# A first-stage subtraction moved behind memsets, a reordered first gate, the first job's splits moved to its second half, and a new order list

## The chip, the cores and the metric

The kernel runs on one core of a Trainium2 chip. The metric is the time of one execution on the device, in microseconds (us); of several runs the median counts. Engines are named as in the profile: PE is TensorE's matmuls (PEld its weight loads), DVE is VectorE, ACT is ScalarE, POOL is GpSimd, SP issues most DMAs.

## What is computed

One block of 2048 tokens with 512 features goes through attention with 32 heads of 16 columns that share one key and one value head, and through a gated feed-forward layer (FFN) with 1376 hidden columns. A gate per token mixes the two.

```python
g = sigmoid((x * gate_w).sum(-1, keepdims=True))
q = (x @ wq).reshape(B, S, 32, 16)           # 32 heads
k, v = x @ wk, x @ wv                        # one head
p = softmax(einsum("bhqd,bkd->bhqk", q, k) * 16 ** -0.5)
a = einsum("bhqk,bkd->bhqd", p, v).reshape(B, S, 512) @ wo
b = (gelu(x @ w_gate) * (x @ w_up)) @ w_down
out = g * a + (1 - g) * b
```

## The kernel before

Everything that needs fp32 accuracy is done as a product of a high and a low half: a tile `t` becomes `hi` (a rounding cast) and `lo = t - hi` (a subtraction), and a product is three matmul passes, high by high, low by high, high by low. Making the two halves is called a split. In the steady part DVE does the cast and POOL the subtraction (`split`, L179 to L184, called by `split_part`, L349).

**First stage (prologue, L159 to L480).** The four groups of 512 tokens are worked one after the other. For each, `first_passes` (L383) runs one 12-matmul pass for the first gate tile `gf` (which also holds the key columns) and one for the first up tile `uf` (value columns), and then 48 matmuls give the queries (`pq`). For the first group, `xh`/`xl` are the halves of its x (four chunks of 128 features), `gh0`/`gl0` those of the weights; `gl0[:, 1]`, the low half for `uf`, is made by POOL at L230, between the memsets of small constants. POOL then clears `hot` (L231 to L233), the tile `zz` (a view of 32 rows of `woh`, L235, L236), and sends `zz` out by four DMAs.

**Steady part (L866 on).** The order of the work on PE is written out by hand, in the list `PLAN`: one line for each FFN or output job, which `play` (L837) reads word by word. `S0`, `S1`, `S2` issue two score matmuls into one of three two-bank PSUM tiles `pair0` to `pair2` and one exponential of both on ACT (L751); `S` issues one score matmul into `single`. The scores of neighbouring heads use the two halves of PE's rows and run side by side. `V`n multiplies n steps of 128 keys by the values (L819; a step is eight PE instructions, on four column groups at once). `H`n opens the line's job in tile `pair`n, `F`n runs n of its steps, each two matmuls on the two halves of PE's rows, and `R` closes it. `T` advances the activation of the last gate job.

A job (`pair_mm`, L507) has two halves, since the two row halves exchange their banks in between: the first matmul of the second half waits for a no-op on POOL (L523), called the relay here, which waits for the last matmuls of the first half. POOL's instructions run in the order of the program, so the relay also stands behind what was queued on POOL ahead of it. After every third step of a job one waiting piece of side work is taken (`slot`, L488): splits for the next job, from the list `todo`, at the third and sixth step of the first half and the third, sixth and ninth of the second; pieces of the softmax's division (`bg`) also at the other places.

A gate job ends in `gelu` (L537): DVE copies `g` from the job's PSUM tile into `gs` (L541), reads `u` from it (L542), does two more operations (L546, L547), ACT a tanh (L550), DVE an operation (L553) and the split of the result (L557, L558). The tile is free for scores again after L542. At the first `V` of all, everything that is left of the activation is flushed, so that ACT's tanh stands ahead of the exponentials that follow. `gates` (L861: one tanh on ACT, then two small DVE operations at L863 and L864) comes once, with the sixth word `S` of the list.

Of the kernel before, what the change touches and what calls it, by code (L numbers as in the profile page):

```python
# [9 lines left out]
F32 = mybir.dt.float32  # L10
# [21 lines left out]
KR = 48  # L32
QK = 51
# [74 lines left out]
]  # L108


@with_exitstack
def mix_kernel(ctx, tc, xT, wq, wo, wf, out):
    nc = tc.nc
    cp = ctx.enter_context(tc.tile_pool(name="cp", bufs=1))
    dr = ctx.enter_context(tc.tile_pool(name="dr", bufs=1, space=DRAM))
    ps_a = ctx.enter_context(tc.tile_pool(name="ps_a", bufs=1, space=PSUM))
    ps_f = ctx.enter_context(tc.tile_pool(name="ps_f", bufs=1, space=PSUM))
    ctx.enter_context(tc.manual_schedule())
# [457 lines left out]
    def gate_job(n):  # L576
        tg, r = chunks[n]

        def begin():
            flush(todo)  # L580
            queue_parts(parts(n))
            return weights_terms(n, 0), weights_terms(n, 1)
# [346 lines left out]
```

## Time and profile before

| | us |
|---|---|
| median of 3 runs | 1224.77 (1224.66 to 1225.57) |
| profiled execution | 1225.59 |
| its span, first to last instruction | 1223.8 |
| PE busy | 1215.6 |
| ACT busy | 1030.4 |
| DVE busy | 528.5 |
| POOL busy | 214.8 |

Times in the trace count from the start of the span. The profile's view of 40 slices shows the granted clock at 9 (90% or more) in all of them. The matmul ends are modelled and overlap: what a matmul costs is the distance from its start to the next one's start, not its own duration.

### The profile page before, as it was taken

How to read it: one execution, taken by the hardware profiler on the slowest of the kernel's cores; microseconds unless marked ns; L12 is line 12 of the kernel's file. 1: busy time of each engine (PE TensorE's matmuls, PEld its weight loads, DVE VectorE, ACT ScalarE, POOL GpSimd, SP SyncE). 2: the span in 40 equal slices, each digit the busy share in tenths (PEclk: the TensorE clock that was granted, in tenths of full speed). 3: DMA queues.
4: the chain of work that ended last, by engine and by line, in shares of the span. 5: the costliest groups of instructions: out<-in, count | busy, mean ns of one | idle time of the engine just before them, and what ended most of it. 6: DMA issues, size and time to landing. Idle time of an engine off the chain costs nothing.

```text
span 1223.8 us, 23880 instructions
## 1 busy us (share of the span) xinstructions
PE 1215.6 (99%) x9742; PEld 684.2 (56%) x9742; DVE 528.5 (43%) x812; ACT 1030.4 (84%) x1301; POOL 214.8 (18%) x188
## 2 busy tenths in 40 slices
PE   9999999999999999999999999999999999999998
PEld 6874555555554565455555555555554555555555
DVE  7773532555245331445426333263616234144524
ACT  5549988888889888989888987889889989799983
POOL 5412201222121100212112110121312011012100
PEclk9999999999999999999999999999999999999999
DMA  8632101212012100112212120112312111011000
GB/s 335 208 131 73 53 8 49 66 53 88 23 53 67 49 32 23 47 52 69 73 36 66 32 75 23 32 38 64 84 43 72 32 58 41 23 40 45 24 1 35
DMA packets 39841, 73.93 MB, mean 60 GB/s; under 512 B 5488, under 2 KB 5744, under 8 KB 39728
## 3 DMA queue, kind: packets, MB, share of 16 engines
q1 hardware_dynamic: 39184, 71.32, 19.1%
q8 instruction: 77, 1.26, 0.4%
q0 software_dynamic: 256, 0.79, 0.2%
q14 instruction: 36, 0.29, 0.1%
q10 hardware_dynamic: 288, 0.26, 0.1%
HBM read 57.41 MB, written 14.94 MB: 59 GB/s over the span
## 4 chain that ended last, share of the span: by engine, by line
PE 92%; ACT 0%; DVE 0%; issue 0%; DVEq 0%; POOL 0%; ACTq 0%; POOLq 0%
PE acc L819 38%; PE pair L515 30%; PE pair L746 20%; PE single L746 3%; PE pair L499 1%; ACT ring L751 0%; PE u L499 0%; DVE acc L628 0%; PE single L499 0%; ACT gs L550 0%; DVE t L553 0%; DVE gs L547 0%; DVE gs L541 0%; DVE t L542 0%; DVEq L925 0%
## 5 line engine op out<-in xcount | busy, mean ns | idle before, releaser
L751 ACT ACTIVATE ring<-pair 128x1024 f32<-128x1024 f32 (+1 forms) x944 | 879.6, 992 | 125.4 <-PE pair L746 123.1
L819 PE MATMUL acc<-ring,v 128*32 128x512 f32 x4096 | 480.9, 597 | 0.0
L746 PE MATMUL pair<-Q,kp 51*128 51x512 f32 x1794 | 389.6, 421 | 0.5 <-ACT ring L751 0.4
L746 PEld LDWEIGHTS pair<-Q,kp 51*128 51x128 f32 x1794 | 201.6, 185 | 203.0 <-ACT ring L751 140.0
L819 PEld LDWEIGHTS acc<-ring,v 128*32 128x32 f32 x4096 | 115.1, 109 | 245.7 <-issue 238.3
L184 POOL TENSOR_TENSOR gl<-st,gh 128x512 fp32r<-128x512 f32 x80 | 112.8, 1430 | 752.2 <-DVE gh L183 433.5
L515 PE MATMUL pair<-xh,gh 64*128 64x512 f32 x624 | 167.5, 393 | 1.1 <-POOLq L523 1.1
L515 PE MATMUL pair<-xh,gl 64*128 64x512 f32 x624 | 167.9, 391 | 0.0
L515 PE MATMUL pair<-xl,gh 64*128 64x512 f32 x624 | 167.1, 391 | 0.0
L751 ACT ACTIVATE ring<-single 128x512 f32<-128x512 f32 x254 | 155.2, 611 | 7.3 <-PE single L746 6.8
L541 DVE COPY gs<-pair 128x512 f32<-128x512 f32 x39 | 27.0, 692 | 207.4 <-PE pair L515 180.9
L515 PEld LDWEIGHTS pair<-xl,gh 64*128 64x128 f32 x624 | 94.5, 186 | 11.0
L746 PE MATMUL single<-Q,kp 51*128 51x512 f32 x254 | 100.4, 395 | 0.0
L515 PEld LDWEIGHTS pair<-xh,gl 64*128 64x128 f32 x624 | 94.8, 186 | 9.5
L515 PEld LDWEIGHTS pair<-xh,gh 64*128 64x128 f32 x624 | 93.9, 186 | 10.3 <-POOLq L523 1.5
L515 PE MATMUL pair<-dl,hh 64*128 64x512 f32 x352 | 91.7, 392 | 0.0
L515 PE MATMUL pair<-dh,hh 64*128 64x512 f32 x352 | 91.2, 393 | 0.0
L515 PE MATMUL pair<-dh,hl 64*128 64x512 f32 x352 | 91.0, 392 | 0.0
L184 POOL TENSOR_TENSOR dl<-st,dh 128x512 fp32r<-128x512 f32 x44 | 57.2, 1302 | 129.7 <-PE pair L746 84.4
L784 DVE RECIPROCAL nz<-n 128x128 f32<-128x128 f32 (+1 forms) x62 | 57.1, 952 | 0.5
L761 DVE COPY n<-acc 128x512 f32<-128x512 f32 x16 | 11.1, 692 | 103.4 <-PE acc L819 103.4
L515 PEld LDWEIGHTS pair<-dl,hh 64*128 64x128 f32 x352 | 51.7, 186 | 6.6 <-issue 0.8
(154 smaller groups left out, 1052.1 us busy)
## 6 DMA issues: line engine op xcount, KB each, us to landing
st<-wf SPq DMA_DIRECT2D x125, 256.0 KB
scr<-q SPq DMA_DIRECT2D x16, 512.0 KB
Q<-scr SPq DMA_DIRECT2D x64, 128.0 KB
Q<-scr SPq DMA_DIRECT2D x64, 64.0 KB
out<-acc SPq DMA_DIRECT2D x16, 256.0 KB
xr<-xT SPq DMA_DIRECT2D x6, 512.0 KB
st<-xT SPq DMA_DIRECT2D x12, 256.0 KB
xr<-xT SPq DMA_DIRECT2D x4, 256.0 KB
```

Source lines behind the costliest of these rows:

```text
L184: eng_l.tensor_sub(lo, src, hi)
L499: nc.tensor.matmul(ps, a, b, start=(first and q == 0), stop=(last and q == len(terms) - 1), skip_group_check=True)
L515: mm = nc.tensor.matmul(ps, a[rs], b[rs], start=(half == 0 and q == 0), stop=(half == 1 and q == len(X) - 1), skip_group_check=True)
L541: nc.vector.tensor_copy(gs, g)
L746: nc.tensor.matmul(ps[:, i * TG : (i + 1) * TG], kp[rs, kc * P : (kc + 1) * P], Q[u][rs, h // 2], start=True, stop=True)
L751: nc.scalar.activation(ring[:, to * TG : (to + b - a) * TG], ps[:, a * TG : b * TG], AF.Exp, bias=0.0, scale=SCALE)
L761: nc.vector.tensor_copy(c0, ac)
L784: nc.vector.reciprocal(z[:, cs], r[:, cs])
L819: nc.tensor.matmul(accp[u][32 * j : 32 * j + 32], vt[:, kc], ring[:, k * TG : (k + 1) * TG], start=(kc == 0), stop=(kc == NKC - 1), skip_g ...
```

## The change

It has five parts.

- POOL's subtraction for `gl0[:, 1]` moves from ahead of `hot` to behind the clearing of `zz`, and that is cut from one memset of four quarters to two of one quarter each (the third quarter is set to 1 as before, the fourth is not sent out and no longer cleared).
- The first gate pass takes its twelve matmuls in the order of a table, `FIRST` of (chunk, kind), where kind 0 is high by high, 1 low weights, 2 low x: the low halves of chunks 1 and 2 come later. All four groups use it.
- The split of `d2` (the down weights of hidden tile 2) is no longer done ahead of the list, but queued with the first gate job (n = 2).
- Two empty pieces are put ahead of it in `todo`, so that this job's three splits (`d2`, and the two of `g3`, the next gate weights) fall to its second half.
- All lines of `PLAN` are other ones; the kinds of jobs and their number (55 `f`, 6 `w`) stay. Lines 1 and 2 are shown.

```diff
+FIRST = [(0, 0), (0, 1), (0, 2), (1, 0), (1, 1), (2, 0), (2, 1), (1, 2), (3, 0), (3, 1), (2, 2), (3, 2)]
 PLAN = [
-    "t: S0 S1 T S",
-    "f: H2 F12 S0 S1 F5 S0 F S F2 S1 F4 R S0 S V S1 S0 T S2 V3 S1 S0 S2 V2 S1",
+    "t: S0 S1",
+    "f: H2 F9 S0 F3 S S1 F2 S0 F S F6 S1 F3 R S0 S V S1 S0 T S2 V3 S1 S0 S2 V2 S1",
...
     make_identity(nc, ident)
-    nc.gpsimd.tensor_sub(gl0[:, 1], g0[1], gh0[:, 1])
     nc.gpsimd.memset(hot, 0.0)
     for r in (QK - 1, 64 + QK - 1):
         nc.gpsimd.memset(hot[:, r : r + 1], 1.0)
     zz = woh[0:H]
-    nc.gpsimd.memset(zz.bitcast(F32), 0.0)
+    nc.gpsimd.memset(zz[:, 0].bitcast(F32), 0.0)
+    nc.gpsimd.memset(zz[:, 1].bitcast(F32), 0.0)
+    nc.gpsimd.tensor_sub(gl0[:, 1], g0[1], gh0[:, 1])
     nc.gpsimd.memset(zz[:, 2].bitcast(F32), 1.0)
...
         if t == 0:
-            seq = [(a, b, c) for c in range(NC) for a, b in kinds]
+            seq = [(*kinds[k], c) for c, k in FIRST]
...
         def begin():
             flush(todo)
+            if n == 2:
+                todo.extend([lambda: None] * 2)
+                queue_parts([("d", 2, 0)])
             queue_parts(parts(n))
...
     chain.pop(0)()
-    split_part(("d", 2, 0))
     defer(5, gates)
```

What stands in a row on POOL in the first stage, after the setting up of `ident` (`gl0` and `gh0` are the weights' halves, `st0` their source, `woh` is where `zz` lies). Before:

```order
masks.py:199 AFFINE_SELECT ident_120<-ident_120 128x128
L230 TENSOR_TENSOR gl0_119<-st0_103,gh0_118 128x512
L231 MEMSET hot_84 1x128
L233 MEMSET hot_84 1x1 x2
L235 MEMSET woh_88 32x2048
L236 MEMSET woh_88 32x512
L238 DMA shs_69<-woh_88 96x1x512 x4
```

and after the change:

```order
masks.py:199 AFFINE_SELECT ident_120<-ident_120 128x128
L231 MEMSET hot_84 1x128
L233 MEMSET hot_84 1x1 x2
L235 MEMSET woh_88 32x512
L236 MEMSET woh_88 32x512
L237 TENSOR_TENSOR gl0_119<-st0_103,gh0_118 128x512
L238 MEMSET woh_88 32x512
L240 DMA shs_69<-woh_88 96x1x512 x4
```

The subtraction has moved behind four memsets, and the large memset has become a quarter, twice.

What stands in a row on DVE around the first gate job of the list (`dh2` and `gh3` are the casts of the splits, `gc` and `gt` the gates, `hh1` and `hl1` the split of hidden tile 1, `gs2` the first operation on this job's result). Before:

```order
L547 SCALAR_TENSOR_TENSOR gs1_1007<-sq_1026,gs1_1007 128x512
L183 CAST dh2_1029<-st_467 128x512
L553 SCALAR_TENSOR_TENSOR t1_1008<-gs1_1007,t1_1008 128x512
L183 CAST gh3_1051<-st_554 128x512
L183 CAST gh3_1051<-st_579 128x512
L863 TENSOR_SCALAR gc_76<-gt_75 128x16
L864 TENSOR_SCALAR gt_75<-gt_75 128x16
L557 CAST hh1_1099<-t1_1008 128x512
L558 TENSOR_TENSOR hl1_1100<-t1_1008,hh1_1099 128x512
L541 COPY gs2_1125<-pair2_1024 128x512
```

and after the change:

```order
L549 SCALAR_TENSOR_TENSOR gs1_1008<-sq_1027,gs1_1008 128x512
L555 SCALAR_TENSOR_TENSOR t1_1009<-gs1_1008,t1_1009 128x512
L868 TENSOR_SCALAR gc_76<-gt_75 128x16
L869 TENSOR_SCALAR gt_75<-gt_75 128x16
L184 CAST dh2_1083<-st_468 128x512
L184 CAST gh3_1097<-st_555 128x512
L184 CAST gh3_1097<-st_580 128x512
L559 CAST hh1_1122<-t1_1009 128x512
L560 TENSOR_TENSOR hl1_1123<-t1_1009,hh1_1122 128x512
L543 COPY gs2_1126<-pair2_1025 128x512
```

The three casts, and with them POOL's three subtractions, have moved behind the gates' two operations, and stand right ahead of `hh1`, `hl1` and `gs2`.

What stands in a row on PE where that job passes from its first half (up to the last `gl2` ahead of a score) to its second (`gh2`, `gl2` are its weights, `Q0` the queries). Before:

```order
L515 MATMUL pair2_1024<-xh0_539,gl2_551 128x512 x2
L746 MATMUL pair0_1022<-Q0_709,kp_71 128x512 x2
L746 MATMUL pair1_1023<-Q0_709,kp_71 128x512 x2
L515 MATMUL pair2_1024<-xh0_539,gh2_550 128x512 x2
L515 MATMUL pair2_1024<-xl0_540,gh2_550 128x512 x2
```

and after the change:

```order
L517 MATMUL pair2_1025<-xh0_540,gl2_552 128x512 x2
L751 MATMUL single_1026<-Q0_710,kp_71 128x512
L751 MATMUL pair1_1024<-Q0_710,kp_71 128x512 x2
L517 MATMUL pair2_1025<-xh0_540,gh2_551 128x512 x2
L517 MATMUL pair2_1025<-xl0_541,gh2_551 128x512 x2
```

Three score matmuls stand between the halves in place of four; the pair `S0` has moved into the first half.

## Rows read from the trace of the kernel before

**Rows 1.** The page, busy time by engine: us, share of the span, instructions.

```profile
PE 1215.6 (99%) x9742; PEld 684.2 (56%) x9742; DVE 528.5 (43%) x812; ACT 1030.4 (84%) x1301; POOL 214.8 (18%) x188
```

**Rows 2.** Waits of PE: engine, tile, line, who ended them; us, times, longest.

```profile
PE pair L515 <- POOLq L523: 1.1, 1, 1.1
PE gf L391 <- DVE xl L184: 0.7, 1, 0.7
```

**Rows 3.** Timeline of PE, first gate: start, us, engine, line, out<-in, count [idle before <-releaser].

```profile
10.41 0.50 PE L391 MATMUL gf<-xl,gh 128*128 128x512 f32 x1 [0.72 <-DVE xl L184]
10.75 1.09 PE L391 MATMUL uf<-xh,gh 128*128 128x512 f32 x4
11.68 1.08 PE L391 MATMUL uf<-xl,gh 128*128 128x512 f32 x4
```

**Rows 4.** Timeline of DVE, same place: the last low half of x, the first of wq.

```profile
8.59 1.77 DVE L184 TENSOR_TENSOR xl<-xr,xh 128x512 fp32r<-128x512 f32 x1
...
10.28 0.68 DVE L184 TENSOR_TENSOR wql<-wqs,wqh 128x512 fp32r<-128x512 f32 x1
```

**Rows 5.** Timeline of POOL, same place.

```profile
8.53 1.28 POOL L230 TENSOR_TENSOR gl<-st,gh 128x512 fp32r<-128x512 f32 x1 [0.41 <-ACT gh L217]
...
10.07 1.80 POOL L235 MEMSET woh<- 32x2048 f32 x1
```

**Rows 6.** Timeline of PE, first job of the list and the words behind it.

```profile
84.07 0.62 PE L746 MATMUL pair<-Q,kp 51*128 51x512 f32 x3
85.75 0.50 PE L515 MATMUL pair<-xh,gh 64*128 64x512 f32 x2 [1.05 <-POOLq L523]
...
90.64 0.96 PE L746 MATMUL pair<-Q,kp 51*128 51x512 f32 x6
91.53 2.78 PE L819 MATMUL acc<-ring,v 128*32 128x512 f32 x24
94.25 1.11 PE L746 MATMUL pair<-Q,kp 51*128 51x512 f32 x4
95.77 0.50 PE L746 MATMUL pair<-Q,kp 51*128 51x512 f32 x2 [0.41 <-ACT ring L751]
```

**Rows 7.** Timeline of DVE, same place.

```profile
86.58 0.23 DVE L863 TENSOR_SCALAR gc<-gt 128x16 f32<-128x16 f32 x1 [0.94 <-ACT gt L862]
...
89.51 0.69 DVE L541 COPY gs<-pair 128x512 f32<-128x512 f32 x1 [0.40 <-PE pair L515]
90.24 0.69 DVE L542 SCALAR_TENSOR_TENSOR t<-pair,gs 128x512 f32<-128x512 f32 x1
```

**Rows 8.** Timeline of ACT, same place.

```profile
84.50 1.94 ACT L751 ACTIVATE ring<-pair 128x1024 f32<-128x1024 f32 x2 [0.41 <-PE pair L746]
86.33 0.22 ACT L862 ACTIVATE gt<-zt 128x16 f32<-128x16 f32 x1
...
92.35 0.63 ACT L550 ACTIVATE gs<-gs 128x512 f32<-128x512 f32 x1 [1.07 <-DVE gs L547]
```

**Rows 9.** Timelines of DVE and POOL where four casts meet two subtractions.

```profile
94.81 0.76 DVE L183 CAST gh<-st 128x512 fp32r<-128x512 f32 x2
95.48 1.50 DVE L183 CAST dh<-st 128x512 fp32r<-128x512 f32 x1
96.90 1.51 DVE L183 CAST woh<-st 128x512 fp32r<-128x512 f32 x1
...
95.37 2.76 POOL L184 TENSOR_TENSOR gl<-st,gh 128x512 fp32r<-128x512 f32 x2 [7.34 <-PE pair L746]
```

**Rows 10.** Timeline of PE in the steady part.

```profile
510.39 1.92 PE L819 MATMUL acc<-ring,v 128*32 128x512 f32 x16
512.24 0.96 PE L746 MATMUL pair<-Q,kp 51*128 51x512 f32 x6
513.13 2.78 PE L819 MATMUL acc<-ring,v 128*32 128x512 f32 x24
```

**Rows 11.** Timeline of PE, the warm-up at the start.

```profile
1.22 5.51 PE L196 MATMUL pw<-warm 128*128 128x512 bf16 x14 [1.22 <-DVE kmx L197]
```

120 rows, old and new, of the table PLAN are left out of this document.

## The prediction

> **What bounds the kernel now.** First the page: PE is busy for 99% of the span [rows 1], so a change is worth what it takes from PE's own row of work or from its few waits. The list of PE's waits names two worth a word [rows 2]: 1.1 us for the relay on POOL and 0.7 us for a low half of x. Matmuls overlap, so "busy" hides slow spacing as well; for that I went through the timeline from start to start. Three places stand out: the end of the first gate [rows 3], the first job of the list [rows 6], where PE loses time twice, and the regular cost of a change between scores and values [rows 10]. Behind the first 100 us the list of waits has nothing, and PE's spacing is regular.
>
> **Part 1: POOL's subtraction, and the order of the first gate.** The last matmul of the first gate starts at 10.41, and the first of the next pass at 10.75 [rows 3]. It waits for the last low half of x, which DVE starts at 8.59 and ends at 10.36, in 1.77 us [rows 4]. The same operation on wq takes 0.68 beside a long memset of POOL [rows 4, 5]. The difference is POOL's subtraction, 8.53 to 9.81 [rows 5]: DVE's ends 0.55 after it, so DVE did not work until POOL had finished. Without it beside it, DVE ends at about 9.27 (the one ahead of it still has to end), and the gate's last matmul starts at 9.33: 1.08 us earlier. The new order matters for what stands ahead of that. Before, the eleventh matmul ended at 9.69 (10.41 less the wait of 0.72) and so started near 9.3; by the old order the twelfth could not start ahead of 9.53. With the late low halves put back, the eleventh comes earlier and the twelfth goes as soon as its data is there. So this part is **-1.08** (bounds 0.88 and 1.1).
>
> What hides the moved step: POOL was free at 8.12 (it idled 0.41 before 8.53). The `hot` memsets take some 0.4, two quarters of the 1.80 us memset about 0.9, so the subtraction runs from about 9.4 to 10.7. `uf` needs it at its third group of four, 8 x 0.23 us behind the earlier start of 9.67: 11.5. It now meets DVE's first low half of wq, which ends at about 11.2 in place of 10.96; the queries' matmuls begin at about 12.4 and find it there. The last memset and the four DMAs behind it leave earlier than before.
>
> The Trainium skill (page "SBUF — State Buffer", section "Who interferes with whom") has a rule that speaks against such a move: an operation of DVE with two inputs in SBUF is shut out for the whole of a GpSimd operation that reads SBUF, and the reverse, by who came first. It says that a memset, which only writes, does not do this to a subtraction. The 0.68 beside the memset bears this out; by a rule under which any work of POOL blocked, this part would bring 0.2 in place of 1.08.
>
> **Part 2: the first job.** Before, PE goes through the first half of job 2, issues four scores (three of them from 84.07 on) and then waits until 85.75 for the relay [rows 6], which stands on POOL behind the splits. With those moved to the second half, the relay has nothing ahead of it. The half ends at the same place (both lists have issued the same number of matmuls by then), three scores follow (0.35 us), and the second half starts at about 84.4: 1.3 us earlier.
>
> I do not count this as won, because of what the splits now stand in front of. On DVE they are behind `gc` and `gt`, and directly ahead of `hh1`, `hl1` and the first operation of the gelu, `gs2`. `gc` waits for ACT's tanh `gt`, which started at 86.33, right behind two exponentials begun at 84.50 [rows 8]. In the new list the first of the two comes earlier and a single lies between: it can start at about 85.9 (bounds 85.5 and 86.3). With two small operations the first cast starts on DVE at about 86.4.
>
> From there a row shows how three casts and two operations go with POOL's subtractions between them. Four casts that started at 94.81 had the third and fourth at 1.50 us, not 0.4 [rows 9]: the third ended 0.28 after POOL's first subtraction, the fourth 0.28 after its second, at 98.41, which is 3.60 after the first cast's start. The two engines took turns. Here a third subtraction follows: it worked 1.15 us in its turn (from the end of the cast at 96.98 to 98.13), and the fifth operation on DVE, the subtraction `hl1`, ends 0.55 later [rows 4, 5]: 3.60 + 1.15 + 0.55 = 5.30 us. So `gs2` starts at 86.4 + 5.3 = 91.7 in place of 89.51 [rows 7], **2.15 us later**.
>
> Who waits for it: the tanh of this job, at 94.5 in place of 92.35 [rows 8], and behind it on ACT, in order, the exponentials of the next `S1`, `S0`, `S2`. And PE, twice. `S2` is to reuse the job's tile, which is free after the second operation: 90.24 + 0.69 + 2.15 = 93.1 [rows 7]. PE, which came there at about 91.2 (the third pair behind 90.64 [rows 6]), is 1.3 us ahead, at about 89.9, and waits 3.2 us. Then, behind three steps of values, the next `S1`, `S0`, `S2` wait for the exponentials, as they did before (from 94.25 to 95.77, where 0.7 would do [rows 6]). The last of them starts at 95.77 + 2.15 = 97.9. The gain at the relay is thus swallowed, and the place where PE is held by ACT comes later by **+2.15** (bounds 1.7 and 2.6, by those of ACT's tanh). Counted from the start of the list.
>
> **Part 3: the rest of the list.** Per line the words are other ones, the work is the same. I counted the two lists. Groups of value steps: 200 before, 198 after; a step costs 0.86 (2.78 - 1.92 for one more), a group of two 1.85 from start to start, so a group costs 0.13 beyond its steps [rows 10]. Stretches of scores alone between two such groups: 111 and 107; six scores cost 0.89, at 0.233 a pair 0.70, so 0.19 each beyond the pairs [rows 10]. Stretches with job steps: 89 and 91, at about the same 0.2. Stretches with an odd number of matmuls, which leave one row half empty for a slot: 8 and 6, 0.12 each. The sum is -2 x 0.13 - 4 x 0.19 + 2 x 0.2 - 2 x 0.12 = -0.86; with 0.25 for the mixed stretches -0.76. I take **-0.8**. A list of other words can also bring a wait that no line of before has, or lose one: 0, with 1.1 on either side, the longest wait that is listed [rows 2]. In both lists the shortest distance from a job's end to the reuse of its tile is about 1.9 us, so I see no new place of the kind of part 2. The tail is the same: 36 matmuls hide the last division as before.
>
> **Sum.** Against the profiled execution, 1225.59: -1.08 + 2.15 - 0.8 = +0.27, 1225.86. The median lies 0.82 below that execution, so the forecast is **1225.0**: no difference that can be told (a measurement of this kernel can tell about 0.2%, 2.4 us).
>
> **Rivals.**
>
> *A: the turns do not happen, and the relay's gain stays.* If the splits get through ahead of the gelu, the list gains 1.3 us in part 2: 1224.77 - 1.08 - 1.3 - 0.8 = 1221.6, faster by 0.26%. For it: POOL is idle for long around, and `gs2` was held by PE, not by DVE, in the trace of before (0.40 idle [rows 7]). Against it: DVE runs in order, so `gs2` cannot pass the casts, and each row of a cast beside a subtraction shows the full wait. 0.15.
>
> *B: the long wait costs PE its clock.* At the start of the trace 14 matmuls of 512 columns take 5.51 us [rows 11], about 0.4 us each, which is the level of 1.2 GHz; later ones come 0.23 apart [rows 3]. A wait of 3.2 us would be three times the longest of before. If PE falls to the lower level there and needs as long as at the start, five us go at half speed: +2.5, 1227.5, slower by 0.22%. It decides only if the wait is long enough, and nothing in this trace shows how long that is. The Trainium skill (page "TensorE: Matmul & The Clock Gate", section "Why this matters for your kernels") warns that idle gaps between bursts of matmuls bring the engine back to its slower clock; no run here shows it yet. 0.08.
>
> *C: the first part's gain is given back,* because POOL's subtraction now delays `uf` or the halves of wq by about its own 1.28 us. That takes back the 1.08: 1226.1. Against it: 0.8 us of slack at `uf`. 0.07.
>
> **Chances and range.** The forecast has 0.70, with its own range 1223.5 to 1226.5 (bounds of part 2 and of the small waits). Faster by over 0.2% (below 1222.3): A, and a little of the forecast's lower end, 0.18. Slower (above 1227.2): B and a little of the upper end, 0.11. Within: 0.71. The range that leaves out no more than 2 in 10 has to reach A: 1221.3 to 1226.8.
>
> **What would show it.** Right: the last low half of x takes 0.7 in place of 1.77, and `uf` starts near 9.7; no wait for the relay in the first job; `hl1` ends some 5.3 us after the first cast of `dh2`; PE waits some 3 us on DVE at the first `S2` behind the first job, and that job's tanh starts some 14 us behind the first score. Wrong: no wait there and a quarter of a per cent gained (A), matmuls 0.43 us apart behind it (B), or a new wait at `uf` (C). The sum fails where the new list has waits that its words don't show.

## The result, and the profile after the change

The changed kernel takes **1227.98 us** (median of 15 runs, 1226.84 to 1231.69), the kernel before 1224.87 (15 runs of the same comparison). The ratio is 1.0026, with an interval of 1.0018 to 1.0034: slower by a quarter of a per cent, where the forecast said no difference and its range ended at 1226.8. The profiled execution took 1227.78, with a span of 1226.0.

PE's busy time is hardly different from [rows 1], so the page alone does not show the loss. Its first line of busy times after the change:

```profile
PE 1217.2 (99%) x9742; PEld 684.4 (56%) x9742; DVE 530.0 (43%) x812; ACT 1031.1 (84%) x1301; POOL 213.9 (17%) x189
```

PE's waits after the change (engine, tile, line, who ended them; us in total, times, longest), to be held against [rows 2]:

```profile
PE pair L751 <- DVE t L544: 3.0, 1, 3.0
```

The waits for the relay on POOL and for the low half of x are gone, and one of 3.0 us has come, on DVE's second operation of the gelu: the wait that the prediction had put at 3.2.

**First stage** (timelines of PE, DVE and POOL after the change: start, us, engine, line, out<-in, count), against [rows 3 to 5]:

```profile
8.93 0.90 PE L393 MATMUL gf<-xl,gh 128*128 128x512 f32 x2
9.66 1.08 PE L393 MATMUL uf<-xh,gh 128*128 128x512 f32 x4
...
7.89 1.38 DVE L185 TENSOR_TENSOR xl<-xr,xh 128x512 fp32r<-128x512 f32 x2
...
9.34 1.29 POOL L237 TENSOR_TENSOR gl<-st,gh 128x512 fp32r<-128x512 f32 x1
```

DVE's last two low halves of x end at 7.89 + 1.38 = 9.27, and the second pass starts at 9.66: 1.09 earlier than the 10.75 of [rows 3]. This is what part 1 forecast for this trace.

**First job** (timelines of PE and DVE after the change), against [rows 6, 7]:

```profile
83.24 0.59 PE L517 MATMUL pair<-xh,gh 64*128 64x512 f32 x2
...
88.26 0.74 PE L751 MATMUL pair<-Q,kp 51*128 51x512 f32 x4
92.00 0.80 PE L751 MATMUL pair<-Q,kp 51*128 51x512 f32 x2 [3.01 <-DVE t L544]
92.73 5.35 PE L824 MATMUL acc<-ring,v 128*32 128x512 f32 x24
98.01 0.97 PE L751 MATMUL pair<-Q,kp 51*128 51x512 f32 x6
...
85.05 0.18 DVE L868 TENSOR_SCALAR gc<-gt 128x16 f32<-128x16 f32 x1 [1.83 <-ACT gt L867]
```

The job's second half starts at 83.24 without a wait, so the relay's gain is there. Then PE waits 3.01 us, and something follows that [rows 6] does not have: the 24 value instructions take 5.35 us in place of 2.78. The chain of waits of this stretch (start, us, what) names the cause of the wait, piece by piece:

```profile
85.34 0.42 DVE dh L184
85.76 1.77 DVE gh L184 x2
87.53 1.44 DVE hh L559
...
88.99 1.63 DVE hl L560
90.62 0.61 DVE gs L543
...
91.26 0.70 DVE t L544
```

From the first cast at 85.34 to the end of `hl` at 90.62 are 5.28 us; the prediction's sum of POOL's turns was 5.30. The cause of the 5.35 us is in the view by stretches of time (stretch, its length, busy time and count of PE, PEld, DVE, ACT, POOL, then PEclk, the granted TensorE clock, DMA share, GB/s):

```profile
90.00:92.00 2.00, 0.00 (x0) 0.00 (x0) 1.97 (x4) 0.00 (x0) 0.07 (x1) 0.80 0.29 96
92.00:94.00 2.00, 2.00 (x10) 0.69 (x14) 1.24 (x2) 0.63 (x2) 0.00 (x0) 0.50 0.00 0
94.00:96.00 2.00, 2.00 (x12) 0.39 (x8) 1.90 (x4) 2.00 (x4) 0.00 (x0) 0.50 0.47 130
96.00:98.00 2.00, 2.00 (x12) 0.20 (x4) 2.00 (x4) 0.74 (x1) 1.62 (x2) 0.50 0.00 1
98.00:100.00 2.00, 2.00 (x22) 0.91 (x22) 1.42 (x1) 1.45 (x3) 1.13 (x1) 0.99 0.46 131
```

From 90 to 92 PE does nothing, the granted clock falls to 0.5, the lower level of 1.2 GHz, before that stretch is over (its mean is 0.80), and comes back near 98. That is rival B.

### The profile page after: what moved, and what is told of

Same layout as the page of the kernel before. It is cut to its first block, busy times and chain, and to the rows that moved or that the text cites. A ratio compares the mean times of both kernels' runs of the same rounds, so it can differ in the third digit from the quotient of the medians.

```text
span 1226.0 us, 23878 instructions
## 1 busy us (share of the span) xinstructions
PE 1217.2 (99%) x9742; PEld 684.4 (56%) x9742; DVE 530.0 (43%) x812; ACT 1031.1 (84%) x1301; POOL 213.9 (17%) x189
## 4 chain that ended last, share of the span: by engine, by line
PE 92%; DVE 1%; ACT 0%; DVEq 0%; issue 0%; ACTq 0%
PE acc L824 38%; PE pair L517 29%; PE pair L751 20%; PE single L751 3%; PE pair L501 1%; ACT ring L756 0%; PE u L501 0%; DVE acc L633 0%; PE single L501 0%; DVE gh L184 0%; DVE hl L560 0%; DVE hh L559 0%; DVE t L544 0%; DVEq L929 0%; ACT gs L552 0%
## 5 line engine op out<-in xcount | busy, mean ns | idle before, releaser
L756 ACT ACTIVATE ring<-single 128x512 f32<-128x512 f32 x260 | 159.7, 614 | 8.8 <-PE single L751 8.3
L517 PEld LDWEIGHTS pair<-dh,hh 64*128 64x128 f32 x352 | 51.0, 186 | 7.3 <-issue 1.7
L751 PEld LDWEIGHTS single<-Q,kp 51*128 51x128 f32 x260 | 48.1, 185 | 12.3 <-ACT ring L756 4.2
```

Source lines behind the costliest of these rows:

```text
L517: mm = nc.tensor.matmul(ps, a[rs], b[rs], start=(half == 0 and q == 0), stop=(half == 1 and q == len(X) - 1), skip_group_check=True)
L751: nc.tensor.matmul(ps[:, i * TG : (i + 1) * TG], kp[rs, kc * P : (kc + 1) * P], Q[u][rs, h // 2], start=True, stop=True)
L756: nc.scalar.activation(ring[:, to * TG : (to + b - a) * TG], ps[:, a * TG : b * TG], AF.Exp, bias=0.0, scale=SCALE)
```

## The experiments

**Theory 1** after this reading: the first stage's part brings 1.1, the list 0.5 to 0.8; the first job loses 2.15 by DVE's turns with POOL, and 1.5 to 1.7 more because PE's clock falls in the wait. **Rival:** the loss lies elsewhere, in the list's other words or in what the first stage's part triggers later. The first four kernels take the change apart. In the comparisons below the kernel before has a median of 1224.53 to 1224.59, 0.3 less than the 1224.87 beside the changed kernel. A difference from the changed kernel's 1227.98 is uncertain by that much, so the difference that is left when each kernel is held against its own kernel before (the changed one is 3.1 us above it) is given with it.

**The first stage's part alone**, on the kernel before:

```diff
-    nc.gpsimd.tensor_sub(gl0[:, 1], g0[1], gh0[:, 1])
     nc.gpsimd.memset(hot, 0.0)
...
-    nc.gpsimd.memset(zz.bitcast(F32), 0.0)
+    nc.gpsimd.memset(zz[:, 0].bitcast(F32), 0.0)
+    nc.gpsimd.memset(zz[:, 1].bitcast(F32), 0.0)
+    nc.gpsimd.tensor_sub(gl0[:, 1], g0[1], gh0[:, 1])
...
-            seq = [(a, b, c) for c in range(NC) for a, b in kinds]
+            seq = [(*kinds[k], c) for c, k in FIRST]
```

> The kernel before with only the first two parts: POOL's subtraction behind the memsets, the zz memset cut in two, and the table for the first gate. Theory 1 (the loss of the changed kernel sits in the first job alone, the first stage gains what its trace shows): uf starts near 9.67, 1.1 us earlier than 10.75, and the whole execution is 1.1 us faster than before, 1223.8. Theory 2 (the loss is spread; what the first stage gains is given back at a later wait): within 0.3 us of before.

Measured: 1224.43 us (1224.03 to 1227.87), the kernel before 1224.53; ratio 1.0002 (0.9993 to 1.0011), which is not exactly the ratio of the two medians (0.9999). There is no gain that can be told, though its trace has the second pass at 9.66 as the full change has:

```profile
9.66 1.09 PE L393 MATMUL uf<-xh,gh 128*128 128x512 f32 x4
```

Theory 1 is wrong here by 1.0 us: it had 1.1 of gain, and 0.1 came.

**The first job's splits alone** (with the first two lines of the new list), on the kernel before:

```diff
             flush(todo)
+            if n == 2:
+                todo.extend([lambda: None] * 2)
+                queue_parts([("d", 2, 0)])
             queue_parts(parts(n))
...
-    split_part(("d", 2, 0))
     defer(5, gates)
```

> The kernel before with only the splits of the first job moved to its second half, with the first two lines of the list that belong to it. Theory 1 (the three splits queue ahead of the job's gelu on DVE, PE waits some 3.4 us for the job's tile and falls to its lower clock): no wait for the relay, hl1 ends 5.3 us after the first cast, PE waits 3 us on DVE at the first S2, low clock for some 7 us, 3.8 us slower than before, 1228.7. Theory 2 (the first job is not the cause): the relay's 1.2 us are gained or nothing moves, 1223.6 to 1225.

Measured: 1228.04 us (1227.06 to 1228.90), ratio 1.0028 (1.0017 to 1.0039). The whole loss, and a little more, is in this part: 3.5 above the kernel before, where the full change is 3.1 above its own. Its trace has the same wait of PE, and a fall of the clock behind it (PE, then one line of the view by stretches):

```profile
92.16 0.79 PE L749 MATMUL pair<-Q,kp 51*128 51x512 f32 x2 [3.11 <-DVE t L542]
92.88 3.94 PE L822 MATMUL acc<-ring,v 128*32 128x512 f32 x24
```

```profile
94.00:96.00 2.00, 2.00 (x16) 0.44 (x12) 1.75 (x4) 2.00 (x4) 0.00 (x0) 0.68 0.44 128
```

The clock is back before 96 here, about half as long at 0.5 as after the change, where some 7 us were expected, and the values take 3.94 in place of 5.35. This profiled execution, 1227.06, is the shortest of the seven.

**The rest of the list alone** (its first two lines as before):

> The kernel before with only lines 3 to 62 of the new list; the first two lines and the splits of the first job as before. Theory 1 (the list saves two groups of value steps and some half slots): 0.5 to 0.8 us faster, 1224.1 to 1224.4, granted clock 1.000. Theory 2 (the new lines bring waits or slow spacing of their own): 1 to 3 us slower, 1226 to 1228.

Measured: 1224.02 us (1223.51 to 1225.08), ratio 0.9994 (0.9985 to 1.0003): 0.5 less than the 1224.53 beside it. The sign and roughly the size agree, though the interval takes in no change.

**The full change with the first job as before** (the diff of the second kernel undone, the first two lines of the list as before):

> The changed kernel with the first job as before: d2 split ahead of the list, no empty pieces, the first two lines of before. The rest of the change stays. Theory 1: the sum of the first stage and the list, 1.6 to 1.9 us faster than before, 1223.0 to 1223.3, no fall of the clock, the relay's wait of 1.1 us back. Theory 2: still slower than before, 1225.5 to 1228.

Measured: 1224.05 us (1223.55 to 1227.26), ratio 0.9998 (0.9989 to 1.0007). The first job's 3.9 us (3.6 against its own kernel before) are gone, but what is left is the list's 0.5 and nothing of the first stage.

**Where the 1.1 us of the first stage are.** The kernel with the new list alone has the first stage of before, and its trace shows no stall there. Its DVE, POOL and PE:

```profile
7.89 1.38 DVE L184 TENSOR_TENSOR xl<-xr,xh 128x512 fp32r<-128x512 f32 x2
...
8.65 1.77 POOL L230 TENSOR_TENSOR gl<-st,gh 128x512 fp32r<-128x512 f32 x1 [0.53 <-ACT gh L217]
...
9.96 1.07 PE L391 MATMUL uf<-xh,gh 128*128 128x512 f32 x4
```

In [rows 4, 5] POOL started its subtraction at 8.53, ahead of DVE's at 8.59, and DVE took 1.77. Here POOL, which had to wait for ACT until 8.65, comes second, and it is POOL's operation that takes 1.77 while DVE's ends at 9.27. With the same code of the first stage, 0.12 us decide who waits, and only DVE's wait is on PE's path: the second pass starts at 9.96, not at 10.75. The Trainium skill (page "SBUF — State Buffer", section "Who interferes with whom") says that of the two engines the one that issues first has the shared port for its whole operation, and that the order of issue decides which of them blocks; these two traces agree, and are the two orders of one first stage: DVE takes 1.77 where POOL came first, and POOL 1.77 where DVE did. New theory: the profiled execution of before lost a race that most executions win. To test it, the last low half was made late in the kernel before, so that DVE loses each time:

```diff
     for c in range(1, NC):
+        if c == NC - 1:
+            nc.vector.memset(warm, 0.0)
+            nc.vector.memset(warm, 0.0)
         split_x(order[0], c)
```

> The kernel before, with two small memsets of a tile that is no longer read put on DVE ahead of the last low half of x, so that this subtraction starts some 0.3 us later. The question is why the first stage's part alone brought nothing. Theory 1 (a race that the profiled execution lost): in most executions of the kernel before DVE takes the last low half ahead of POOL's subtraction, as in the traces of the two kernels that left the first stage as it was (DVE at 8.59, POOL at 8.65 and 8.73; 0.68 us); only where POOL comes first (8.53) does it take 1.77 us. Then the memsets make DVE lose always: the low half ends some 0.55 behind POOL's operation, near 10.5, the second pass starts near 10.8 in place of 9.75 to 9.97, and the time is 1225.5 to 1225.7, 1.0 over the kernel before. Rival (the gain of the first stage is given back later): the second pass starts as late as that, and the time stays at 1224.5. Rival (the two memsets alone): 0.3 more, 1224.8.

Measured: 1225.56 us (1224.39 to 1225.83, nine of eleven above 1225.5), the kernel before 1224.56 beside it: 1.0 more; ratio 1.0006 (0.9997 to 1.0015). Its DVE, POOL and PE:

```profile
9.25 1.12 DVE L184 TENSOR_TENSOR xl<-xr,xh 128x512 fp32r<-128x512 f32 x1
...
8.54 1.29 POOL L233 TENSOR_TENSOR gl<-st,gh 128x512 fp32r<-128x512 f32 x1 [0.41 <-ACT gh L220]
...
10.76 1.09 PE L394 MATMUL uf<-xh,gh 128*128 128x512 f32 x4
```

DVE's operation ends at 10.37 although it started at 9.25, 0.7 later than in [rows 4], where it ended at 10.36: its end is set by POOL's, at 9.83. The time is that of the profiled execution of before, 1225.59. Of the 116 executions of the kernel before in all comparisons, 11 were above 1225.2 and the others near 1224.6: by their times about one in ten loses the race, and the profile had caught one of these.

**Does PE's idle time cost the clock?** Twelve matmuls of the scores' shape, with unused results, were put where PE waits:

```diff
-    "f: H2 F9 S0 F3 S S1 F2 S0 F S F6 S1 F3 R S0 S V S1 S0 T S2 V3 S1 S0 S2 V2 S1",
+    "f: H2 F9 S0 F3 S S1 F2 S0 F S F6 S1 F3 R S0 S V S1 S0 T W12 S2 V3 S1 S0 S2 V2 S1",
...
+            elif t[0] == "W":
+                for _ in range(k):
+                    nc.tensor.matmul(single, kp[0:QK, 0:P], Q[0][0:QK, 0], start=True, stop=True)
```

> The changed kernel, with 12 more matmuls (scores' shape, into the one-bank tile, results unused) on PE ahead of the pair that waits for the first job's tile, where PE idled 3 us. They take 2.8 us, so the pair starts at 92.0 as before. Theory (the idle time costs PE its clock): no fall of the granted clock, the 24 value instructions behind it take 2.8 us in place of 5.35, and the time is 1.7 us under the changed kernel, 1226.2, with less spread. Rival (the place where PE is held is set by DVE and ACT alone, the slower matmuls are hidden by ACT): as the changed kernel, 1227.7.

Measured: 1226.25 us (1226.00 to 1228.29), ratio 1.0014 (1.0005 to 1.0023): 1.7 under the changed kernel (1.4 against its own kernel before) with more work on PE, as the theory said. But the profiled execution (1226.61, among the longer ones) still shows a fall, later and shorter. Its PE, then its view by stretches:

```profile
88.84 3.05 PE L851 MATMUL single<-Q,kp 51*128 51x512 f32 x12
92.06 0.50 PE L751 MATMUL pair<-Q,kp 51*128 51x512 f32 x2 [0.16 <-DVE t L544]
92.48 4.48 PE L824 MATMUL acc<-ring,v 128*32 128x512 f32 x24
```

```profile
90.00:92.00 2.00, 1.90 (x9) 1.16 (x7) 1.97 (x4) 0.00 (x0) 0.12 (x1) 1.00 0.34 111
92.00:94.00 2.00, 1.95 (x11) 0.57 (x15) 1.29 (x3) 0.58 (x2) 0.00 (x0) 0.68 0.00 0
94.00:96.00 2.00, 2.00 (x16) 0.62 (x12) 1.85 (x4) 2.00 (x4) 0.00 (x0) 0.50 0.44 129
```

PE was idle for 0.16 us, and the clock fell all the same. So being busy was not enough there. The same with all 128 rows in use in place of 51:

```diff
-                    nc.tensor.matmul(single, kp[0:QK, 0:P], Q[0][0:QK, 0], start=True, stop=True)
+                    nc.tensor.matmul(single, *X[0], start=True, stop=True)
```

> As the kernel with 12 filling matmuls of scores' shape, but each of the 12 on all 128 rows of PE in place of 51 (a weight tile of the first job by its x, results unused). The former took the 1.7 us off that the theory named, yet its profiled execution shows a granted clock of 0.5 for 3.41 us right behind the filler, though PE had not idled. Theory 1 (the clock falls by how little PE works there, not by the wait itself; 51 rows without a neighbour on the other half are little): with full rows no fall in the profile, the 24 value instructions in 2.8 us, 1226.1 and a narrower spread. Theory 2 (what the filler does is of no matter; the fall behind it is chance, or comes from the V and S instructions that follow): falls as before in about a third of the executions, 1226.25.

> The kernel with 12 filling matmuls on all 128 rows, again: of its first six executions three took 1226.0 to 1226.4 and three 1229.7 at a mean clock of 0.998, and the profiled one was of the first kind. If the profiled one is of the second kind this time, its trace shows where: theory 1, a stretch at 0.5 somewhere else than behind the filler (there it was 1.0 throughout); theory 2, behind the filler, as in the kernel with 51 rows, with 24 value instructions in 4 to 5.4 us.

Measured: of the first six executions three took 1226.0 to 1226.4 and three 1229.7 to 1229.8 (median 1228.04, ratio 1.0029, 1.0017 to 1.0041), so theory 1's 1226.1 and its narrower spread did not come there. Of eleven more, ten took 1225.65 to 1226.56 and one 1229.68 (median 1226.24, ratio 1.0016, 1.0007 to 1.0025). Both profiled executions were of the short kind (1226.13 and 1226.01), and neither shows a fall. That fits theory 1; but if a fall came in a third of the executions, as theory 2 has it, two profiles without one would be no surprise. PE of the first of them:

```profile
88.94 3.01 PE L851 MATMUL single<-xh,gh 128*128 128x512 f32 x12
92.05 0.50 PE L751 MATMUL pair<-Q,kp 51*128 51x512 f32 x2
92.49 2.78 PE L824 MATMUL acc<-ring,v 128*32 128x512 f32 x24
...
95.92 0.50 PE L751 MATMUL pair<-Q,kp 51*128 51x512 f32 x2 [0.23 <-ACT ring L756]
96.84 0.50 PE L751 MATMUL pair<-Q,kp 51*128 51x512 f32 x2 [0.41 <-ACT ring L756]
97.26 1.92 PE L824 MATMUL acc<-ring,v 128*32 128x512 f32 x16
```

This gives the price of the fall. The pair behind the wait starts at the same time as after the change (92.05 against 92.00), the values take 2.78 in place of 5.35, and the next group of values starts at 97.26 in place of 98.91: **1.65 us**. It is less than the 2.57 of the values, because at the full clock PE then waits for ACT (0.23 and 0.41), and at the lower one ACT has caught up. The two profiled executions differ by as much (1227.78 and 1226.13). The price hangs on how long the clock stays down: in the profile with 51 rows, whose values took 4.48, the next group starts at 97.77, only 0.51 later than here. The executions at 1229.7 were not met in a profile; where their 3.5 us lie stays open (below).

**DVE's turns with POOL.** The next kernel keeps the splits where the change puts them, but no longer lets the gates' two operations hold them up:

```diff
-    defer(5, gates)
+    defer(16, gates)
```

> The changed kernel, with the gates' tanh and its two small DVE operations 11 slots later, so that DVE does not wait for them ahead of the three casts. Theory (the casts' late start and the turns with POOL hold the first job): the casts start near 83.2 in place of 85.3, the split of hidden tile 1 ends near 88.6 in place of 90.6, PE waits 1.1 us in place of 3.0, too little for the clock to fall, and the time is 1224.2 (1223.6 to 1224.8), 3.5 under the changed kernel. Rival (the clock falls at a wait of about 1 us as well): a granted clock of 0.5 behind it and 1225.9. Rival (the turns are not the cause): as the changed kernel, 1227.7.

Measured: 1224.08 us (eleven executions at 1223.36 to 1226.13; a twelfth took 3048.55, of which there is no trace), ratio 0.9998 (0.9989 to 1.0007): 3.9 under the changed kernel (3.6 against its own kernel before). Its PE and DVE:

```profile
89.90 0.50 PE L751 MATMUL pair<-Q,kp 51*128 51x512 f32 x2 [0.84 <-DVE t L544]
90.33 2.78 PE L824 MATMUL acc<-ring,v 128*32 128x512 f32 x24
...
83.19 0.42 DVE L184 CAST dh<-st 128x512 fp32r<-128x512 f32 x1
...
88.44 0.68 DVE L543 COPY gs<-pair 128x512 f32<-128x512 f32 x1
```

The casts start 2.15 us earlier, the copy out of the job's tile 2.11 earlier, the wait shrinks from 3.01 to 0.84, and the clock stays up. The turns are still there (5.3 us from the first cast to the copy) and still hold PE, by these 0.84 us; the next kernel, with no split in front of the copy, is 1.4 us faster.

**A version that uses this.** The down weights are split ahead of the list again, and the two splits of the next gate weights come behind the gelu's first four operations, where DVE waits for ACT's tanh:

```diff
             flush(todo)
-            if n == 2:
-                todo.extend([lambda: None] * 2)
-                queue_parts([("d", 2, 0)])
-            queue_parts(parts(n))
+            if n > 2:
+                queue_parts(parts(n))
...
             gelu(n, z, y)
             advance(3)()
+            if n == 2:
+                for p in parts(n):
+                    split_part(p)
...
+    split_part(("d", 2, 0))
     defer(5, gates)
```

> The changed kernel, with the split of the down weights ahead of the list again, and the two splits of the next gate weights behind the first four operations of the first job's activation, where DVE waits for ACT. So neither the relay nor the job's first operations stand behind a split. Theory: no wait for the relay, the first copy out of the job's tile at about 87.1 (88.6 where the first job is as before), no wait of PE at the pair behind it, no fall of the clock; 1.1 us under the changed kernel with the old first job (1224.05), so 1222.9, faster than both. Rival (the splits now hold the tail of the activation, or the next job's start): a wait of PE on POOL or DVE at the next job near 97, and 1224 or more.

> The version with the two splits behind the gelu's first operations, as run before (1222.69), now beside its twin with the old first stage. Theory: 1222.7 again; one or two of its executions 1.5 to 3.7 us longer if the new first stage brings these, none if they were chance.

Measured: 1222.69 us, ratio 0.9988 (0.9979 to 0.9997), and again 1222.71, 0.9989 (0.9980 to 0.9998): faster than the kernel before, by 1.9 us in the medians and by 0.11 to 0.12% in these ratios, and than the changed one by 5.3 us (5.0 against its own kernel before). The full change with the first job as before was 0.5 under the kernel before; this one is 1.4 under that. Its job's second half starts at 83.25, where the other's, behind a wait for the relay, starts at 84.81. Two of the second eleven executions were 2.0 and 3.9 us above the median, as were two of the first eleven, by 1.6 and 3.5. Its PE and DVE:

```profile
83.25 0.59 PE L517 MATMUL pair<-xh,gh 64*128 64x512 f32 x2
...
88.27 0.97 PE L752 MATMUL pair<-Q,kp 51*128 51x512 f32 x6
89.18 2.78 PE L825 MATMUL acc<-ring,v 128*32 128x512 f32 x24
...
87.03 0.69 DVE L543 COPY gs<-pair 128x512 f32<-128x512 f32 x1 [0.53 <-PE pair L517]
...
90.53 1.61 DVE L555 SCALAR_TENSOR_TENSOR t<-gs,t 128x512 f32<-128x512 f32 x1
92.17 1.38 DVE L559 CAST hh<-t 128x512 fp32r<-128x512 f32 x1
```

There is neither a wait for the relay nor one for the tile; DVE, not PE, is early at 87.03. The turns with POOL now stretch the tail of the activation (1.61 and 1.38), for which nothing on PE waits. Last, the same with the first stage of before:

> The version with the two splits behind the gelu's first operations, and the first stage as it was before the change. Theory (the first stage's part saves only where POOL's subtraction would have come first): 1222.8 to 1223.0, within 0.3 of the version with the new first stage (1222.7), with single executions about 1 us longer. Rival (the first stage's part is worth its 1.08 once the first job no longer takes it): 1223.8. Of the executions that are 1.5 to 3.7 us over their kernel's median: there are 11 among 62 of the kernels with the new first stage, and none among 75 with the old one and an undisturbed first job; if the new first stage brings them, none is seen here.

Measured: 1222.72 us (1222.46 to 1223.77), ratio 0.9986 (0.9977 to 0.9995), the same as with the new first stage; none of its executions is more than 1.05 above the median. Its profiled execution happens to be the longest of the eleven, 1223.77, and shows why: it is one that lost the race.

```profile
7.89 2.48 DVE L184 TENSOR_TENSOR xl<-xr,xh 128x512 fp32r<-128x512 f32 x2
```

The two low halves end at 10.37 here, not at 9.27, and this execution is 1.05 us above the median.

## Why the prediction was wrong

Two steps of the sum failed. It had no term for PE's clock behind the wait of 3.2 us that it forecast itself (this stood outside the sum, as rival B at 0.08); in the trace the fall costs 1.65. And it took one stall off twice, as -1.08 and again as the 0.82 by which the median lies below the profiled execution. Each alone would have left the sum inside the stated range (1226.7 and 1225.9, where the range ended at 1226.8); together they make 1227.5. The mechanisms of parts 1 and 2 came as forecast, and part 3 was over-sized.

**Part 1, in the trace right, in the sum counted twice.** Each step came: the low half ends at 9.27, the last gate matmul and the second pass start 1.09 earlier, POOL's subtraction has slack (its end, 9.34 + 1.29 = 10.63, is ahead of 11.5), and the first low half of wq, at 9.85 + 1.33 = 11.18, is where it was expected. So rival C is out. The step that failed here is the last sentence of the sum: "the median lies 0.82 below that execution". That the profiled execution stood above the median was the very stall that part 1 removes, in an execution that had it where most do not. To take off 1.08 for the stall and then 0.82 for the median took the same time off twice; rival A's sum, which takes 1.08 from the median 1224.77, does so too. Against the median this part is worth about nothing (1224.43 against 1224.53); against the profiled execution it is worth 1.08.

**Part 2, the turns right.** The second half starts without a wait; the three casts, `hh1` and `hl1` take 5.28 us (forecast 5.30); the copy out of the tile starts 1.04 later than in [rows 7], 2.1 later counted from the start of the list, which came 1.1 earlier; PE waits 3.01 (forecast 3.2). With PE kept busy in the wait on all rows, the second job's first values start at 103.55, and in the kernel with the new first stage alone, at 101.41: 2.14, where the forecast had 2.15 (its own times, 91.7 - 89.51, make 2.19). The rows of the two kernels:

```profile
103.55 0.64 PE L824 MATMUL acc<-ring,v 128*32 128x512 f32 x4
```

```profile
101.41 1.92 PE L821 MATMUL acc<-ring,v 128*32 128x512 f32 x16
```

After the change these values start at 105.20, so the fall of the clock adds 105.20 - 103.55 = 1.65:

```profile
105.20 1.92 PE L824 MATMUL acc<-ring,v 128*32 128x512 f32 x16
```

**Rival B happened, and had been given 0.08.** Its mechanism, a wait long enough for the clock to fall, was named, with the page of the Trainium skill that warns of idle gaps between bursts of matmuls ("TensorE: Matmul & The Clock Gate", section "Why this matters for your kernels"); this trace agrees, with 3.0 us idle and the granted clock at 0.5 before they were over and behind them. The forecast itself contained the wait of 3.2 us, and no row of before spoke for a clock that outlasts such a wait, so 0.08 had nothing behind it. Its price, 2.5, was too high by 0.85: that sum let PE run at half speed for five us and forgot that PE waited for ACT there anyway. Its time, 1227.5, is within 0.5 us of the measured one by luck: the price that was too high made up for the 0.82 taken off twice.

**Part 3, right in sign, over-sized.** 0.5 in place of 0.8, by the kernel with the list alone; of this the interval leaves much open.

**Rival A is out**: the turns happened in every kernel that put the splits in front of the gelu. The relay's gain of 1.3 that it counted was there to be had all the same, once the splits stood behind the gelu's first operations (1.4 above).

**The sum again**, against the profiled execution: 1225.59 - 1.08 + 2.14 + 1.65 - 0.5 = 1227.80; the profiled execution of after took 1227.78. Against the median of before, where the race is mostly won: 1224.87 + 2.14 + 1.65 - 0.5 = 1228.16; measured 1227.98. The miss of 2.9 us (1227.98 against 1225.04) is thus 1.65 for the clock, 0.82 for the stall taken off twice and 0.3 for the list; the 0.2 left is as much as the median of after lies above its profiled execution.

## What to carry to other kernels

Where the profiled execution lies off the median, look first for a wait in it that depends on which of two engines came first by a tenth of a microsecond: it may be the whole difference, and a change that removes it is then worth little in the median, where most executions never had it. Work for which two engines take turns, as DVE and POOL did in the splits (5.28 us for five operations of DVE), should stand where its engine waits anyway, not in front of an operation that frees a tile for PE; where three splits stood in the first job decided over some 5 us here, more than all other parts of the change together. A forecast that holds a long wait of PE (3.0 us here) should carry a price for the clock in its main sum, less what PE would have waited for anyway behind it.

## What the runs showed of the hardware that was not expected

- A tenth of a microsecond decides which of DVE and POOL waits for the other: with DVE's subtraction at 8.59, POOL's start at 8.53 makes DVE's take 1.77 us in place of 0.68, and its start at 8.65 makes POOL's take 1.77 in place of 1.28. The lost race costs about 1.05 us; by their times 11 of 116 executions of the kernel before lost it.
- The granted clock fell within 3.0 and 3.1 us without matmuls, not behind a wait of 0.84, and in one profiled execution behind twelve matmuls of 51 rows that left PE idle for only 0.16 us; behind twelve of 128 rows it did not fall in two. What decides between these is not settled by so few profiles. After the change the clock stayed at 0.5 about twice as long as in the kernel with 51 rows, and that cost more (1.65 us against 0.51).
- Kernels with the new first stage and without the long wait have single executions 1.5 to 3.9 us above their median, the longest at a mean clock of 0.998: 14 of 83 (without the one of 3048.55). The changed kernel itself has 3 of 15, at 1229.93 to 1231.69. Of 149 executions with the old first stage and no long wait, none is over 1.4 above. But for the first six of the kernel with 128 rows the medians do not feel it, and no profile met one, so where this time lies, and which of the first stage's edits brings it, stays open.
